# A planned opening in which GpSimd waits for VectorE's preceding instruction on the shared port, with another operation for the softmax sum's epsilon and new plan constants

## The chip, the core and the metric

The kernel runs on one core of one Trainium2 chip. Its engines are TensorE (PE in the profile, its weight loads PEld), VectorE (DVE), ScalarE (ACT), GpSimd (POOL) and SyncE (SP, which here only issues transfers). The metric is the device time of one execution in microseconds, as a median of several runs.

## What is computed

Windowed attention over 8 batches of 8 heads, 576 positions and 64 columns, and behind it a feed-forward block over all 4608 tokens:

```python
scores = scale * np.matmul(q, k.transpose(0, 1, 3, 2))
...
mask = (rel >= 0) & (rel < window)                 # window = 128
scores = np.where(mask, scores + bias[None], -1000000000.0)
scores = scores - np.max(scores, axis=-1, keepdims=True)
attn = np.exp(scores)
attn = attn / (np.sum(attn, axis=-1, keepdims=True) + 1e-09)
return np.matmul(attn, v).astype(np.float32)
...
h = x @ w_in                                       # 512 -> 2048
g = h * (1.0 / (1.0 + np.exp(-1.702 * h)))
return (g @ w_out).astype(np.float32)              # 2048 -> 512
```

## The kernel before

**Products.** Data are fp32. Apart from batch 0's attention, each product is made of three products of fp32r parts: an operand is rounded ("high" part) and the remainder is kept as a "low" part (names `K`, `Q`, `VV`, `xl`, `gl`, `pl`, and the second half of a weight tile `w`). So each operand takes a cast (`copy_on`, L439) on ACT or DVE and a subtraction (`less_on`, L442) on POOL or DVE. Weights come from HBM as raw words and are decoded first: two ACT instructions (L515, L517), two DVE ones (L519, L522), then cast and subtraction.

**Attention.** A unit is two blocks of 128 query rows (or one of 64). `scores` makes s on PE (L693 in batch 0, L696 behind it), `biased` (L711, DVE) adds mask and slope and finds the minimum, `exponents` (L723, ACT) makes exp in place and lets ACT add up each row, so that the sum lies in `sums`. `normal` adds 1e-9 to the sums (L732, DVE tensor_scalar), takes the reciprocal (L734) and multiplies the rows with it (L743 on ACT, L745 on DVE or POOL). `flip` transposes on PE (L766), `high` and `low` empty that, `mix` multiplies with v (L805, L811) and `sum_up` writes x. In batch 0 the tiles `work`, `turned` and `numbers` (minima, sums and reciprocals of 8 heads) lie in places that later hold weights.

**Feed-forward.** A job takes 256 tokens through 16 slices of the hidden width: `up` makes h (L880), ACT makes tanh (L888), DVE the gate (L889), then `gh` and `gl`, and `down` adds into `acc` (L904). The first job stops after eight slices while weights still arrive, and is finished as the third.

**The order.** All this is first recorded as operations with an engine, a cost in ns, buffers and dependences (`Plan.add`). Some may go to either of two or three engines (`ways`). [...] The constants on top steer it: how late an engine may be before another gets the work (`LAX`), how far weights are fetched (`FETCH_AHEAD`), at which tick the first weight is decoded (`DECODE_TICK`), behind which exponent later decodes stand (`GATE`). The order comes out as the program's order on each engine. On the chip each engine takes its instructions in this order, and semaphores hold them for data alone: nothing holds POOL to the planned order against DVE. Where PE would have nothing to do in the plan, `spin` (L486) puts dummy products of the identity, up to the first operation on `acc0`. What the plan doesn't reach is emitted by `rest` in the order in which it was recorded.

Of the kernel before, what the change touches and what calls it, by code (L numbers as in the profile page):

```python
# [14 lines left out]
AF = mybir.ActivationFunctionType  # L15
ALU = mybir.AluOpType
PSUM = bass.MemoryType.PSUM

# [3 lines left out]
P = 128  # L22
# [10 lines left out]
SCALE = 0.125  # L33
BIG = 3.0e38
FAR = 1.0e37
DEPTH = 3
FETCH_AHEAD = 5
DECODE_AHEAD = 1
F0 = 8
SLACK = 2  # L40
DECODE_TICK = 7
AHEAD = 3000
GATE = 6
READY = {"PE": 1600, "DVE": 4400, "ACT": 700, "POOL": 2700, "SP": 700}
HOP = {"PE": 220, "ACT": 60, "DVE": 60, "POOL": 60, "SP": 60}
CUT = 130000
WARM = 7000
LAX = {"w": 1500, "hi": 800, "lo": 2000, "gl": 150, "cast": 300, "xl": 300, "p": 300}
RATE = 330
# [136 lines left out]


class Part:

# [21 lines left out]
class Op:  # L211


    def __init__(self, n, eng, run, ns, lag, port):
        self.n, self.eng, self.run, self.ns, self.lag, self.port = n, eng, run, ns, lag, port
        self.ways = {eng: (ns, port)}
        self.waits, self.next, self.ready, self.opens, self.bufs = 0, [], 0, [], []
        self.bytes = 0
        self.start = None
        self.before = 0  # L220


class Plan:
# [56 lines left out]
    def order(self, until):  # L280

        free = dict(READY)
        port = 0
        wire, landed = 0, []
# [12 lines left out]
        while True:  # L297
            best = None
            for e in ENGINES:
# [21 lines left out]
                if pick:  # L321
                    at = max(pick[0], port) if pick[2].ways[e][1] else pick[0]
                    if best is None or (at, pick[0]) < best[:2]:
                        best = (at, pick[0], pick[2], e)
# [15 lines left out]
            if op.port:  # L340
                port = at + op.ns
            end = at + op.ns + (30 if op.eng == "POOL" else op.lag)
            if op.bytes:
# [56 lines left out]
def tile_kernel(ctx: ExitStack, tc: tile.TileContext, q0, k0, v0, qT, kT, v, w_in, w_out, out):  # L400
# [61 lines left out]
    bias = [const.tile([P, 2 * P], BF16, name=f"bias{h}") for h in range(H)]  # L462

    def tables():


        make_identity(nc, ident)
        rel_i = raw.tile([P, 2 * P], I32, name="rel_i", tag="rq_0")
        nc.gpsimd.iota(rel_i, pattern=[[-1, 2 * P]], base=P, channel_multiplier=1)
# [77 lines left out]
    def home(shape, name):  # L547
        return buf(const, shape, F32, homes.pop(), name=name)
# [108 lines left out]
    def small(u, i, name):  # L657
        if first(u):
            return Part(numbers, (u.n, i), lambda t: t[:, 3 * u.n + i])
        return buf(att, [P, 2], F32, name, 3)  # L660

    def scores(u):
# [34 lines left out]

        add("PE", run, ns, 165, r=reads if u.whole else [u.Q, u.K1, u.K2], w=[u.s], chain="scores")

# [18 lines left out]
    def exponents(u):  # L718
        u.sums = small(u, 1, "sums")
        for e, b in enumerate(u.blocks):  # L720
            def run(e=e, b=b):
                live = b.p.t[:b.rows, b.live:b.end]
                nc.scalar.activation(  # L723
                    live, live, AF.Exp, bias=u.mins.t[:b.rows, e:e + 1], scale=-1.0,
                    accum_out=u.sums.t[:b.rows, e:e + 1])
            gates.append(add(
                "ACT", run, 300 + 0.8 * (b.end - b.live), 95, r=[u.mins.key_at(e)], w=[b.p.key_at(), u.sums.key_at(e)], chain="exp"))

    def normal(u, on_act=False):
        u.rec = small(u, 2, "rec")  # L730
        rows, ne = u.blocks[0].rows, len(u.blocks)
        add("DVE", lambda: nc.vector.tensor_scalar(u.rec.t[:rows, :ne], u.sums.t[:rows, :ne], 1e-9, None, ALU.add),  # L732
            70, 90, r=[u.sums.key_at()], w=[u.rec.key_at()], port=True, chain="rec")
        add("DVE", lambda: nc.vector.reciprocal(u.rec.t[:rows, :ne], u.rec.t[:rows, :ne]),  # L734
# [250 lines left out]
    turned = [home([P, 2, 4 * P], f"turned{i}") for i in range(4)]  # L985
    numbers = home([P, 24, 2], "numbers")
    load_part(0, T, "ACT")
# [67 lines left out]
    def emit(op):  # L1055
        op.run(op.eng) if len(op.ways) > 1 else op.run()

    done = plan.order(CUT)
# [64 lines left out]
```

## Time and profile before

| | |
|---|---|
| runs | 1058.71, 1064.49, 1058.6 us; median 1058.71 |
| profiled execution | 1059.04 us, its span 1057.3 us |
| PE busy | 1046.5 us, 99% of the span |
| DVE, ACT, POOL busy | 717.9, 612.5, 590.2 us |
| DVE, ACT, POOL busy, first 130 us | 112.9, 113.2, 64.3 us |
| DMA, first 40 us | 306 to 410 GB/s; 75 GB/s over the span |

The profile is one execution. Busy time is time in which an engine has an instruction under way; for PE the ends are modelled, so full windows can hold waits. A row of groups gives line, engine, operation, the tiles out<-in, the shapes, the count, then busy us and mean ns of one, then the idle time ahead of them and what ended it. A row of the waits reads: who <- for whom: us in total, times, longest.

### The profile page before, as it was taken

What the parts mean: (1) busy time and instruction counts of PE and PEld (TensorE: products, weight loads), DVE (VectorE), ACT (ScalarE), POOL (GpSimd) and SP (SyncE); (2) the same over time, 40 slices, a digit from 0 to 9 for tenths busy, and PEclk for the clock granted to TensorE, in tenths of its full rate; (3) what the DMA queues carried; (4) which work ended last, traced back from release to release, by engine and by line L of the source; (5) the groups of instructions that cost most, each with busy time, mean ns of one, the idle gap of its engine ahead of it and who ended that gap; (6) DMA issues with size and microseconds to landing.
All of it is one profiled execution on the core that took longest, in us unless ns stands there. A gap on an engine that the chain in (4) does not pass through costs nothing.

```text
span 1057.3 us, 21848 instructions
## 1 busy us (share of the span) xinstructions
PE 1046.5 (99%) x7054; PEld 941.5 (89%) x7054; DVE 717.9 (68%) x2327; ACT 612.5 (58%) x1823; POOL 590.2 (56%) x877
## 2 busy tenths in 40 slices
PE   9999999999999999999999999999999999999998
PEld 5778889998989999999999998999999999999987
DVE  7889988789887868544767677766878586413221
ACT  7988975666666665534555555655665565322222
POOL 3455666676776665544555666655766565323232
PEclk9999999999999999999999999999999999999999
DMA  9712333323332222211222223222322120000000
GB/s 351 293 56 90 122 88 87 83 82 100 83 94 68 84 69 58 72 43 29 67 63 60 73 62 87 67 68 59 87 67 85 54 81 18 20 1 21 1 21 21
DMA packets 88035, 80.21 MB, mean 76 GB/s; under 512 B 41776, under 2 KB 78128, under 8 KB 87920
## 3 DMA queue, kind: packets, MB, share of 16 engines
q1 hardware_dynamic: 82448, 68.84, 22.1%
q10 hardware_dynamic: 5472, 9.96, 2.6%
q8 instruction: 56, 0.92, 0.4%
q14 instruction: 59, 0.48, 0.2%
HBM read 69.34 MB, written 9.44 MB: 75 GB/s over the span
## 4 chain that ended last, share of the span: by engine, by line
PE 93%; DMA 3%; DVE 2%; issue 1%; POOL 1%; ACT 1%; SPq 0%; DVEq 0%; POOLq 0%
PE h_ps L880 37%; PE acc L904 37%; PE x_ps L811 5%; PE s_ps L696 5%; PE t_ps L766 5%; DMA rw<-w_in 1%; PE x_ps L805 1%; DMA v<-v 1%; PE s_ps L693 1%; DMA rw<-w_out 1%; POOL w L442 0%; DVE pb L745 0%; SPq L416 0%; DVE rec L732 0%; DVE pb L711 0%
## 5 line engine op out<-in xcount | busy, mean ns | idle before, releaser
L880 PE MATMUL h_ps<-xh,w 128*128 128x256 f32 x2304 | 368.1, 284 | 1.3 <-DVE g L889 1.1
L442 POOL TENSOR_TENSOR gl<-g,gh 128x256 fp32r<-128x256 f32 x275 | 206.3, 751 | 270.5 <-ACT gh L439 210.3
L880 PEld LDWEIGHTS h_ps<-xh,w 128*128 128x128 f32 x2304 | 327.0, 188 | 29.0 <-DVE g L889 2.1
L904 PE MATMUL acc<-w,gh 128*128 128x512 f32 x1152 | 325.7, 399 | 0.0
L889 DVE SCALAR_TENSOR_TENSOR g<-g,h_ps 128x256 f32<-128x256 f32 x288 | 119.2, 414 | 179.6 <-ACT g L888 178.3
L888 ACT ACTIVATE g<-h_ps 128x256 f32<-128x256 f32 x288 | 109.7, 381 | 201.2 <-PE h_ps L880 184.3
L904 PEld LDWEIGHTS acc<-w,gh 128*128 128x128 f32 x1152 | 195.8, 188 | 25.9 <-issue 0.3
L439 ACT CAST gh<-g 128x256 fp32r<-128x256 f32 x288 | 116.7, 405 | 145.8 <-DVE g L889 135.6
L880 PE MATMUL h_ps<-xl,w 128*128 128x256 f32 x1152 | 194.3, 280 | 0.0
L904 PE MATMUL acc<-w,gl 128*128 128x512 f32 x576 | 187.0, 400 | 0.0
L880 PEld LDWEIGHTS h_ps<-xl,w 128*128 128x128 f32 x1152 | 163.9, 188 | 6.3
L442 POOL TENSOR_TENSOR K<-rk,K 128x384 fp32r<-128x384 f32 (+1 forms) x139 | 126.8, 912 | 73.1 <-ACT Q L439 18.0
L723 ACT ACTIVATE pb<-pb,mins 128x256 f32<-128x256 f32 (+3 forms) x276 | 134.0, 487 | 48.0 <-DVE mins L711 46.3
L711 DVE CUSTOM_DVE_ANT_0 pb<-s_ps,bias 128x256 f32<-128x256 f32 (+2 forms) x304 | 109.3, 378 | 10.7 <-PE s_ps L696 4.4
L745 DVE TENSOR_SCALAR pb<-pb,rec 128x256 f32<-128x256 f32 (+2 forms) x251 | 109.2, 469 | 3.5
L442 POOL TENSOR_TENSOR Q<-rq,Q 64x256 fp32r<-64x256 f32 (+1 forms) x140 | 96.2, 687 | 23.4 <-DVE g L889 3.9
L904 PEld LDWEIGHTS acc<-w,gl 128*128 128x128 f32 x576 | 93.8, 188 | 9.8 <-issue 0.3
L766 PE MATMUL t_ps<-ident,pb 128*128 128x128 f32 (+2 forms) x524 | 94.6, 272 | 0.7 <-DVE pb L745 0.7
L696 PE MATMUL s_ps<-K,Q 128*128 128x256 f32 (+1 forms) x504 | 90.5, 290 | 0.5 <-DVE mins L711 0.4
L732 DVE TENSOR_SCALAR rec<-sums 128x2 f32<-128x2 f32 (+2 forms) x156 | 48.1, 308 | 62.5 <-ACT pb L723 61.4
L785 DVE TENSOR_TENSOR pl<-t_ps,ph 128x512 fp32r<-128x512 f32 (+2 forms) x140 | 84.4, 604 | 4.7 <-ACT ph L439 4.1
L696 PEld LDWEIGHTS s_ps<-K,Q 128*128 128x128 f32 x504 | 74.1, 189 | 6.1 <-DVE mins L711 0.6
(95 smaller groups left out, 1268.6 us busy)
## 6 DMA issues: line engine op xcount, KB each, us to landing
rk<-kT SPq DMA_DIRECT2D x84, 192.0 KB, 2.3
rq<-qT SPq DMA_DIRECT2D x112, 128.0 KB, 2.2
out<-o ACTq DMA_DIRECT2D x36, 256.0 KB, 2.1
rw<-w_in SPq DMA_DIRECT2D x16, 512.0 KB, 8.7
rw<-w_out SPq DMA_DIRECT2D x16, 512.0 KB, 9.6
rk<-kT SPq DMA_DIRECT2D x56, 128.0 KB, 2.0
rv<-v SPq DMA_DIRECT2D x100, 64.0 KB, 2.0
rq<-qT SPq DMA_DIRECT2D x28, 64.0 KB, 1.9
```

What stands on the lines that cost most here:

```text
L439: (nc.scalar.copy if e == "ACT" else nc.vector.tensor_copy)(dst, src)
L442: (nc.gpsimd if e == "POOL" else nc.vector).tensor_tensor(dst, a, b, ALU.subtract)
L696: nc.tensor.matmul(to, u.Q.t[:, q], ks.t[:, k], start=(z == 0), stop=(z == 1))
L711: add("DVE", lambda b=b, e=e, head=head, ra=ra, rb=rb, cs=cs: nc.vector.tensor_tensor_reduce(b.p.t[ra:rb, cs:b.end], u.s.t[ra:rb, e, cs:b. ...
L723: nc.scalar.activation(live, live, AF.Exp, bias=u.mins.t[:b.rows, e:e + 1], scale=-1.0, accum_out=u.sums.t[:b.rows, e:e + 1])
L745: (nc.gpsimd if on == "POOL" else nc.vector).tensor_scalar(live, live, rec, None, ALU.mult)
L766: nc.tensor.transpose(u.t.t[:c.n, w:w + b.rows], b.p.t[:b.rows, col:col + c.n], ident[:b.rows, :b.rows])
L785: add("DVE", lambda m=m, a=a, z=z: nc.vector.tensor_tensor(u.pl.t[:m, a:z], u.t.t[:m, a:z], u.ph.t[:m, a:z].bitcast(F32), ALU.subtract), d ...
L880: nc.tensor.matmul(h.t, w.t[:, z, k * P:(k + 1) * P], x[k].t, start=(part == 0 and k == 0), stop=(part == 2 and k == NC - 1))
L888: add("ACT", lambda: nc.scalar.activation(g.t, h.t, AF.Tanh, scale=0.851), act_psum(T), r=[h], w=[g], shift=-NEXT)
L889: add("DVE", lambda: nc.vector.scalar_tensor_tensor(g.t, g.t, 1.0, h.t, ALU.add, ALU.mult), dve_one(T), r=[h], w=[g], shift=-NEXT)
L904: nc.tensor.matmul(acc.t, g.t[:, t * P:(t + 1) * P], w.t[:, z], start=(f == self.f0 and n == 0), stop=(f == self.f1 - 1 and n == 2))
```

## The change

Four things are changed.

1. `order` remembers the DVE operation on the port that it placed last (`asked`). The first POOL port operation placed behind it starts no earlier than its end plus `BEHIND` = 160 ns in the plan, and in the program gets a semaphore wait on it (`emit`). This holds for the planned part only.
2. Sums and the 1e-9 stand side by side: `sums` gets a second column, set once by two POOL memsets to 1e-9, ACT writes the sum beside it, and a DVE `tensor_reduce` adds the two columns, in place of the tensor_scalar. In the plan this operation no longer counts as one on the port. It is used in the whole program. For all but the first units of batch 0, the sums lie in three fixed slots of one tile (`totals`, class `Fixed`).
3. Scores of odd heads in the first units are booked with 40 ns on PE and 540 ns until their result, where it was their own cost and 165.
4. The constants `FETCH_AHEAD`, `DECODE_TICK`, `GATE` and `LAX` have other values.

```diff
-FETCH_AHEAD = 5
+FETCH_AHEAD = 3
-DECODE_TICK = 7
+DECODE_TICK = 2
+BEHIND = 160
-GATE = 6
+GATE = 10
-LAX = {"w": 1500, "hi": 800, "lo": 2000, "gl": 150, "cast": 300, "xl": 300, "p": 300}
+LAX = {"w": 600, "hi": 800, "lo": 500, "gl": 300, "cast": 100, "xl": 300, "p": 900}
@@ Plan.order
-        port = 0
+        port, asked = 0, None
                     at = max(pick[0], port) if pick[2].ways[e][1] else pick[0]
+                    if e == "POOL" and asked:
+                        at = max(at, asked.start + asked.ns + BEHIND)
             if op.port:
                 port = at + op.ns
+                if op.eng == "DVE":
+                    asked = op
+                elif asked:
+                    op.behind, asked = asked, None
@@ tile_kernel
+    totals = const.tile([P, 3, 2, 2], F32, name="totals")
+        nc.gpsimd.memset(totals[:, :, :, 1], EPS)
+        nc.gpsimd.memset(numbers.t[:, :, 1:3, 1], EPS)
@@ small
-            return Part(numbers, (u.n, i), lambda t: t[:, 3 * u.n + i])
+            return Part(numbers, (u.n, i), lambda t: t[:, u.n, 1:3] if i == 1 else t[:, u.n, i])
+        if i == 1:
+            return Fixed(plan, "sums", 3, lambda at: totals[:, at])
@@ scores
-        add("PE", run, ns, 165, r=reads if u.whole else [u.Q, u.K1, u.K2], w=[u.s], chain="scores")
+        add("PE", run, 40 if early(u) else ns, 540 if early(u) else 165, r=reads if u.whole else [u.Q, u.K1, u.K2], w=[u.s], chain="scores")
@@ exponents
-                    accum_out=u.sums.t[:b.rows, e:e + 1])
+                    accum_out=u.sums.t[:b.rows, e, 0:1])
@@ normal
-        add("DVE", lambda: nc.vector.tensor_scalar(u.rec.t[:rows, :ne], u.sums.t[:rows, :ne], 1e-9, None, ALU.add),
-            70, 90, r=[u.sums.key_at()], w=[u.rec.key_at()], port=True, chain="rec")
+        add("DVE", lambda: nc.vector.tensor_reduce(u.rec.t[:rows, :ne], u.sums.t[:rows, :ne], AX.X, ALU.add),
+            75, 90, r=[u.sums.key_at()], w=[u.rec.key_at()], chain="rec")
@@ emit
+        if op.port and op.start is not None:
+            on = nc.vector.engine if op.eng == "DVE" else nc.gpsimd.engine
+            op.made = next(i for i in reversed(nc.cur_bb.bb.instructions) if i.engine == on)
+            if op.behind:
+                tc.add_manual_dep(op.made, op.behind.made.name, mybir.DependencyInfo(
+                    mybir.DependencyClass.Sync, mybir.DependencyReason.DATA))
```

What this does to the order is seen best on POOL, where the weights of the third to the fifth slice are split. `w` is a weight tile (its subtraction), `wc` the decoded weight, `gl` the gate's low part, `pb` a block of probabilities that is normalised; in brackets stand the engines or transfer queues whose semaphores an instruction waits for. Before:

```order
L442 TENSOR_TENSOR w_2_0_550<-wc_533,w_2_0_550 128x512 [waits DMAHW5_49,Activation_49]
L442 TENSOR_TENSOR w_2_0_575<-wc_565,w_2_0_575 128x512 [waits DMAHW6_49,Activation_49]
L442 TENSOR_TENSOR gl_607<-g_537,gh_599 128x256 [waits PE_49,Activation_49]
L442 TENSOR_TENSOR w_3_0_643<-wc_628,w_3_0_643 128x512 [waits DMAHW7_49,DVE_49]
L442 TENSOR_TENSOR K_0_678<-rk_321,K_0_646 128x384 [waits DMAHW2_49,Activation_49]
L442 TENSOR_TENSOR gl_708<-g_634,gh_697 128x256 [waits PE_49,Activation_49]
L442 TENSOR_TENSOR w_4_0_744<-wc_731,w_4_0_744 128x512 [waits DMAHW1_49,Activation_49]
```

and after:

```order
L464 TENSOR_TENSOR w_2_0_623<-wc_605,w_2_0_623 128x512 [waits DMAHW6_49,DVE_49,Activation_49]
L464 TENSOR_TENSOR w_3_0_658<-wc_648,w_3_0_658 128x512 [waits DMAHW7_49,DVE_49]
L773 TENSOR_SCALAR pb_642<-pb_642,rec_666 128x256 [waits DVE_49,PE_49,Activation_49]
L464 TENSOR_TENSOR w_3_0_699<-wc_688,w_3_0_699 128x512 [waits DMAHW0_49,DVE_49,Activation_49]
L464 TENSOR_TENSOR gl_739<-g_673,gh_732 128x256 [waits DVE_49,PE_49]
L464 TENSOR_TENSOR w_4_0_762<-wc_752,w_4_0_762 128x512 [waits DMAHW1_49,Activation_49]
```

Five of these six rows now wait for DVE, one of seven did before; one subtraction of slice 2 has gone to DVE and a normalisation has come.

On DVE the first unit of batch 0 shows the sum's operation. The ISA rows are `biased` and its read of the minimum. Before:

```order
L711 ISA work_0_135,numbers_136<-s_h_132,bias_75 128x128 [waits DVE_49,PE_49]
L711 ISA numbers_136 128x1
L732 TENSOR_SCALAR numbers_136<-numbers_136 128x2 [waits Activation_49]
L711 ISA work_0_135,numbers_136<-s_h_132,bias_75 128x256
L711 ISA numbers_136 128x1
L734 RECIPROCAL numbers_136<-numbers_136 128x2 [waits DVE_49]
L745 TENSOR_SCALAR work_0_135<-work_0_135,numbers_136 128x128 [waits DVE_49]
```

and after:

```order
L739 ISA work_0_139,numbers_91<-s_h_136,bias_75 128x128 [waits DVE_49,PE_49]
L739 ISA numbers_91 128x1
L739 ISA work_0_139,numbers_91<-s_h_136,bias_75 128x256
L739 ISA numbers_91 128x1
L760 TENSOR_REDUCE numbers_91<-numbers_91 128x2 [waits Activation_49]
L762 RECIPROCAL numbers_91<-numbers_91 128x2 [waits DVE_49]
L773 TENSOR_SCALAR work_0_139<-work_0_139,numbers_91 128x128 [waits DVE_49]
```

The new operation stands one `biased` later, directly ahead of its reciprocal.

On PE, at the scores of the first two heads (`s_ps` and `s_h`), before:

```order
L693 MATMUL s_ps_127<-k_0_107,q_0_109 128x256
L693 MATMUL s_h_132<-k_0_107,q_0_109 128x128
L693 MATMUL s_h_132<-k_0_107,q_0_109 128x256
L693 MATMUL s_ps_141<-k_0_107,q_0_109 128x128
L693 MATMUL s_ps_141<-k_0_107,q_0_109 128x256
```

and after:

```order
L721 MATMUL s_ps_131<-k_0_111,q_0_113 128x256
L721 MATMUL s_h_136<-k_0_111,q_0_113 128x128
L721 MATMUL s_h_136<-k_0_111,q_0_113 128x256
L512 LDWEIGHTS ident
L512 MATMUL idle<-ident 128x256
```

Five such dummy products now stand between the first pair of heads and the second; over the whole program there are 76 where there were 66.

More of the change, by code (lines that the diff above doesn't have):

```diff
@@ L16 @@
 ALU = mybir.AluOpType
+AX = mybir.AxisListType
 PSUM = bass.MemoryType.PSUM
@@ L34 @@
 BIG = 3.0e38
+EPS = 1e-9
 FAR = 1.0e37
 DEPTH = 3
-FETCH_AHEAD = 5
+FETCH_AHEAD = 3
 DECODE_AHEAD = 1
@@ L185, in key_at, with __init__, t @@
         return self, sub
+class Fixed(Buf):
+    def __init__(self, plan, tag, slots, place):
+        super().__init__(plan, None, None, None, tag, slots)
+        self.place = place
+    @property
+    def t(self):
+        return self.place(self.at)
 class Part:
@@ L220, in __init__ @@
         self.before = 0
+        self.behind = self.made = None
 class Plan:
@@ L729, in normal @@
     def normal(u, on_act=False):
-        u.rec = small(u, 2, "rec")
+        u.rec = small(u, 3, "rec")
         rows, ne = u.blocks[0].rows, len(u.blocks)
-        add("DVE", lambda: nc.vector.tensor_scalar(u.rec.t[:rows, :ne], u.sums.t[:rows, :ne], 1e-9, None, ALU.add),
-            70, 90, r=[u.sums.key_at()], w=[u.rec.key_at()], port=True, chain="rec")
+        add("DVE", lambda: nc.vector.tensor_reduce(u.rec.t[:rows, :ne], u.sums.t[:rows, :ne], AX.X, ALU.add),
+            75, 90, r=[u.sums.key_at()], w=[u.rec.key_at()], chain="rec")
         add("DVE", lambda: nc.vector.reciprocal(u.rec.t[:rows, :ne], u.rec.t[:rows, :ne]),
@@ L985, in tile_kernel @@
     turned = [home([P, 2, 4 * P], f"turned{i}") for i in range(4)]
-    numbers = home([P, 24, 2], "numbers")
+    numbers = home([P, H, 4, 2], "numbers")
     load_part(0, T, "ACT")
```

## The prediction

> **What bounds the kernel now.** I read the page's busy shares and its chain, then the windows, then the waits of PE, and last the DVE groups of the opening. Busy shares and the chain by engine:
>
> ```profile
> PE 1046.5 (99%) x7054; PEld 941.5 (89%) x7054; DVE 717.9 (68%) x2327; ACT 612.5 (58%) x1823; POOL 590.2 (56%) x877
> PE 93%; DMA 3%; DVE 2%; issue 1%; POOL 1%; ACT 1%; SPq 0%; DVEq 0%; POOLq 0%
> ```
>
> PE is the bound as a mean. The windows show where it is not alone (columns: length, then busy us of PE, PEld, DVE, ACT and POOL, the granted clock, the DMA share and GB/s):
>
> ```profile
> 40.00:50.00 10.00, 9.84 (x59) 7.65 (x58) 9.34 (x28) 9.89 (x25) 4.21 (x4) 1.00 0.56 221
> 120.00:130.00 10.00, 9.95 (x73) 9.11 (x72) 9.69 (x30) 9.85 (x30) 5.92 (x8) 1.00 0.20 49
> 0.00:130.00 130.00, 126.44 (x796) 98.50 (x797) 112.89 (x351) 113.15 (x308) 64.25 (x76) 0.99 0.51 183
> 260.00:520.00 260.00, 259.18 (x1777) 238.43 (x1776) 183.06 (x606) 148.87 (x457) 157.89 (x244) 1.00 0.24 67
> ```
>
> From 260 to 520 us DVE has 77 of 260 us idle and ACT 111, so there only PE counts, and nothing in this change removes PE work. In the first 130 us DVE and ACT both are busy for 113 us, while POOL is busy for 64. What PE waits for directly is small, in the first 140 us and behind them:
>
> ```profile
> PE s_ps L693 <- DVE numbers L711: 1.0, 1, 1.0
> PE s_ps L693 <- DVE mins L711: 0.7, 1, 0.7
> PE h_ps L880 <- POOL w L442: 0.2, 1, 0.2
> PE h_ps L880 <- DVE g L889: 1.1, 2, 0.8
> PE x_ps L811 <- DVE xf L851: 0.8, 2, 0.4
> PE t_ps L766 <- DVE pb L745: 0.7, 1, 0.7
> ```
>
> The first three are the opening's, the last three are of the rest. More is hidden in fillers, the dummy products of L486, which stand where the planner expects PE to wait, and in modelled matmul ends. The fillers of the first 30 and the next 30 us, and ten in a row:
>
> ```profile
> 0.00:30.00 30.00, 8.47 (x55) 5.42 (x55) 0.94 0.97 357
> 30.00:60.00 30.00, 1.55 (x11) 0.91 (x11) 1.00 0.53 210
> 24.68 1.27 PE L486 MATMUL idle<-ident 128*128 128x256 bf16 x10
> 25.78 0.27 PE L766 MATMUL t_ps<-ident,work 128*128 128x128 f32 x1
> ```
>
> Ten start within 25.78 - 24.68 = 1.10 us, 0.11 us each, so the 66 fillers are some 7.3 us. Whatever this change gives must come out of the opening: out of these fillers and out of the lateness of DVE and ACT.
>
> **The port.** What the new wait is about can be seen at 50.8 us, in the timeline:
>
> ```profile
> 42.50 0.75 DVE L439 CAST w<-wc 128x512 fp32r<-128x512 f32 x2
> 50.83 1.28 POOL L442 TENSOR_TENSOR w<-wc,w 128x512 fp32r<-128x512 f32 x1 [2.86 <-ACT w L439]
> 50.87 1.52 DVE L439 CAST w<-wc 128x512 fp32r<-128x512 f32 x1
> ```
>
> and in the chain of work that ended last:
>
> ```profile
> 50.96 1.43 DVE w L439
> ...
> 52.79 1.14 PE s_ps L693 x6
> ```
>
> Two casts in a row take 0.75 us, 0.375 each. The one at 50.87 began 0.04 us behind a POOL subtraction and took 1.52, until just after POOL's end at 52.11. It lost 1.15 us, and it is on the chain: PE's scores start behind it at 52.79 (the 0.7 us wait above). POOL itself had idled 2.86 us before and was in no hurry.
>
> **The change part by part.** First the size of all such losses on DVE in the first 145 us, from the groups kept apart by form (mean ns behind the comma):
>
> ```profile
> L522 DVE SCALAR_TENSOR_TENSOR wc<-rw,w_ps 128x512 int32<-128x512 int32 x32 | 21.4, 675 | 0.0
> L889 DVE SCALAR_TENSOR_TENSOR g<-g,h_ps 128x256 f32<-128x256 f32 x24 | 9.9, 412 | 0.9 <-ACT g L888 0.7
> L442 DVE TENSOR_TENSOR gl<-g,gh 128x256 fp32r<-128x256 f32 x13 | 8.5, 653 | 0.9 <-PE acc L904 0.9
> L442 DVE TENSOR_TENSOR w<-wc,w 128x512 fp32r<-128x512 f32 x8 | 6.0, 749 | 0.0
> L439 DVE CAST w<-wc 128x512 fp32r<-128x512 f32 x10 | 5.6, 568 | 0.0
> L732 DVE TENSOR_SCALAR rec<-sums 128x2 f32<-128x2 f32 x16 | 3.6, 227 | 1.4 <-ACT pb L723 1.2
> L734 DVE RECIPROCAL rec<-rec 128x2 f32<-128x2 f32 x16 | 2.5, 155 | 0.0
> L732 DVE TENSOR_SCALAR numbers<-numbers 128x2 f32<-128x2 f32 x8 | 2.4, 305 | 0.5 <-ACT work L723 0.5
> L442 DVE TENSOR_TENSOR xl<-x,xh 128x256 fp32r<-128x256 f32 x2 | 2.0, 978 | 0.0
> L745 DVE TENSOR_SCALAR pb<-pb,rec 128x192 f32<-128x192 f32 x4 | 1.8, 448 | 0.0
> L745 DVE TENSOR_SCALAR pb<-pb,rec 64x192 f32<-64x192 f32 x1 | 1.4, 1365 | 0.0
> ```
>
> L889 and L522 are two-operand operations of the same shapes as gl, xl and w that read PSUM, and never stretch. Above them lie gl with 13 x (653 - 412) = 3.1 us, xl with 2 x (978 - 412) = 1.1, w with 8 x (749 - 675) = 0.6, the casts with 10 x (568 - 375) = 1.9, one normalisation with 1365 - 448 = 0.9. That is 7.6 us. The sum's addition of 1e-9, against the reciprocal of the same two columns: 16 x (227 - 155) + 8 x (305 - 155) = 2.3 us.
>
> (a) The addition becomes a tensor_reduce. The trace has no such instruction. From below, it costs a reciprocal's 155 ns; two more elements to read cost (412 - 155) / 254 = 1 ns each by the slope between L734 and L889. From above, it costs the addition's 227 and 305 and gains nothing. I take 157. What comes back is then all of the 2.3 us on DVE. One such loss stands on the chain, behind the planned part:
>
> ```profile
> 143.47 0.79 DVE rec L732
> 144.28 0.18 DVE rec L734
> ```
>
> That is 0.6 us beyond a bare one. I take 1.0 us for the end time, between 0 and 2.3. In the rest of the program 132 more such additions get shorter, but DVE idles there and PE's waits for it sum to 2.6 us in the three rows above. I take 0, and if they all went, 2.6.
>
> (b) POOL waits for DVE's preceding port instruction. In the order, 49 of the planned POOL rows wait for DVE where 18 did. [...] Bounds are 1.1 and 7.6 us; I take a third, 2.5, because DVE is over nine tenths busy in the two windows shown, yet PE's direct waits for it in the opening are 1.7 us. The price is on POOL: 31 added waits, each with whatever is queued behind it there, subtractions for w and gl that PE's products need. POOL idles 66 of the first 130 us, and PE waited for it 0.2 us. I take 0.5 us. If that cover were gone, 31 waits of about the 0.45 us of a DVE port operation would be 14 us on POOL, and a third of them on PE's path 4.7.
>
> [...]
>
> (c) The new constants move work. In the order ACT has 17 instructions fewer, DVE 16 more (10 subtractions come from POOL, 16 copies and casts from ACT, 10 normalisations leave for POOL and ACT), POOL 3 more, two of them memsets. Means of what leaves ACT:
>
> ```profile
> L439 ACT CAST gh<-g 128x256 fp32r<-128x256 f32 x21 | 8.5, 403 | 0.6 <-DVE g L889 0.5
> L439 ACT COPY turned<-t_ps 128x384 f32<-128x384 f32 x6 | 2.8, 475 | 2.4 <-PE t_ps L766 2.4
> ```
>
> 17 x 0.42 = 7.1 us off ACT. ACT is at 9.85 or more in two of the fourteen windows of 10 us up to 140 us, and only there do I count it: 7.1 x 2 / 14 = 1.0 us of gain. The bounds are 4 us of gain (over half reaches the end) and 5.2 us of loss (DVE, below). The transfers cost nothing: SP's queue holds the same loads in the same order for its first 78 rows. The two memsets on POOL come ahead of the mask tables:
>
> ```profile
> 2.91 1.70 DVE L478 TENSOR_SCALAR bias<-rel 128x256 bf16<-128x256 f32 x8 [0.97 <-POOL rel L473]
> 0.74 0.20 POOL masks.py:197 MEMSET ident<- 128x128 f32 x1 [0.29 <-POOLq L1119]
> 5.33 0.29 DVE L711 CUSTOM_DVE_ANT_0 work<-s_ps,bias 128x128 f32<-128x128 f32 x1 [0.71 <-PE s_h L693]
> ```
>
> At 0.2 us each at most, 0.4 us are hidden: its tables are made at 4.61, and DVE then waits 0.71 us for PE's first scores. Ten more fillers, 76 for 66, would be 1.1 us of PE, but fillers stand where PE waits anyway; 0, at worst 1.1.
>
> **The sum.** -1.0 - 2.5 + 0.5 - 1.0 = -4.0 us. The profiled execution took 1059.0 us (1057.3 in the span, 1.7 around it), 0.3 above the runs' median of 1058.7; so 1055.0 on its own scale and 1054.7 as a median. What a measurement of this kernel tells from no change is about 1%, 10.6 us: below 1048.1 or above 1069.3.
>
> **The rivals.**
>
> No change, 1057 to 1060, about 1058.5. [...] Against it: the cast at 50.87 is on the chain and POOL's idle time of 2.86 us in front of it wasn't. This also covers the case that the change doesn't do what it says, because the added waits are nearly always over when POOL gets its data.
>
> DVE becomes the bound of the opening, slower, about 1064. Ten subtractions at about 0.6 us (between the 412 and the 675 ns above) and 16 copies and casts at about the 0.375 of a bare cast come to DVE, 10 normalisations at 0.45 leave it: 6.0 + 6.0 - 4.5 = 7.5 us more. At 9.69 of 10 in 120 to 130 us it has no room there. If the collisions stay and only the 2.3 us of (a) come back, DVE ends 5.2 us later: 1058.7 + 5.2 = 1063.9. It decides once DVE's windows up to 130 us stand at 9.7 or more; for it speaks that row, against it the 17 us that DVE idles over the 130.
>
> The opening follows its plan and all stretching goes: 9.9 us of DVE, 1058.7 - 9.9 = 1048.8. For it: DVE and ACT are both nearly full and feed each other, so that one late instruction makes the other late. Against it: most of the stretched groups can be cases in which POOL was rightly first.
>
> **How the numbers follow.** The forecast, 1052 to 1057, has 0.50; no change 0.22; DVE or POOL late, above 1060, 0.14; nearly all recovered, below 1052, 0.14. The range goes from 1049.0, the full recovery, to 1061.5, half of the slower case's 5.2 us above the median, and leaves about 0.15 out. Faster by over 1% needs more than the whole port loss, 0.05; slower by over 1% would need twice DVE's added work, 0.02; within 1%, 0.93.
>
> **What would show it.** In the changed profile: tensor_reduce at 150 to 165 ns in the opening and behind it; the DVE groups of gl, w and the cast nearer to 412, 675 and 375; more POOL idle time released by DVE, and PE's waits for POOL still under 1 us; ACT's windows at 40 and 120 us below 9.8; PE's span from 260 us on as before. I am wrong if the stretched groups stay as they are while the time falls (then moved work did it), if PE comes to wait for POOL's w or gl by microseconds, or if DVE's windows reach 9.7 and the end is later.

## The result and the profile after

The changed kernel took 1052.82 us as a median of six runs (1052.34 to 1053.83), the kernel before 1059.43 on the same chip (six runs). The ratio is 0.9932 with a 95% interval of 0.9913 to 0.9951. One execution of the kernel before took 1064.49 us and the other five 1058.2 to 1060.2, while none of the changed kernel's stands apart, so the ratio says a little more than the medians. By these it is 6.6 us faster, where 4.0 were forecast; the time lies in the range, and most of the gain comes from a place that the prediction had ruled out.

Busy shares and the chain by engine of the changed kernel (profiled execution 1052.34 us, span 1050.6):

```profile
PE 1041.9 (99%) x7064; PEld 938.8 (89%) x7064; DVE 695.9 (66%) x2343; ACT 613.7 (58%) x1806; POOL 586.7 (56%) x880
PE 96%; DVE 2%; ACT 1%; issue 0%; POOL 0%; DVEq 0%; POOLq 0%; ACTq 0%
```

PE is busy for 4.6 us less, with ten products more. DVE is busy for 22 us less. Two stretches of the prediction, and one near the end of the program:

```profile
40.00:50.00 10.00, 10.00 (x63) 7.63 (x61) 8.56 (x28) 9.11 (x24) 5.12 (x6) 1.00 0.53 211
120.00:130.00 10.00, 9.90 (x67) 8.60 (x66) 9.83 (x35) 8.75 (x27) 5.93 (x10) 1.00 0.21 56
950.00:1040.00 90.00, 90.00 (x587) 81.86 (x586) 22.69 (x49) 25.59 (x65) 27.07 (x37) 1.00 0.04 13
```

and the last of these in the kernel before:

```profile
950.00:1040.00 90.00, 90.00 (x581) 81.29 (x580) 22.26 (x48) 25.29 (x64) 26.82 (x37) 1.00 0.03 13
```

The last rows are the surprise. Near the end there is no attention, both kernels run the same products in the same order, PE is full, and the clock is 1.00. Still PE begins 587 products in 90 us, where it began 581: 1% more. What PE waits for, in the first 140 us (first row) and behind them:

```profile
PE idle L512 <- POOL ident masks.py:199: 1.4, 1, 1.4
...
PE t_ps L794 <- DVE pb L773: 0.9, 2, 0.6
PE s_ps L724 <- DVE mins L739: 0.9, 2, 0.7
PE h_ps L908 <- DVE xh L461: 0.5, 1, 0.5
PE x_ps L839 <- DVE xf L879: 0.2, 1, 0.2
```

The wait for the identity, 1.4 us, is there in both kernels. The opening's other waits of 1.9 us are gone; those behind it sum to 2.5 us, about what they were (2.6). And the DVE groups of the first 145 us that answer to the prediction's:

```profile
L464 DVE TENSOR_TENSOR w<-wc,w 128x512 fp32r<-128x512 f32 x13 | 10.7, 824 | 1.4 <-ACT w L461 1.4
L464 DVE TENSOR_TENSOR gl<-g,gh 128x256 fp32r<-128x256 f32 x14 | 6.1, 434 | 0.4 <-ACT gh L461 0.3
L461 DVE CAST w<-wc 128x512 fp32r<-128x512 f32 x6 | 2.7, 457 | 0.0
L760 DVE TENSOR_REDUCE rec<-totals 128x2 f32<-128x4 f32 x15 | 2.3, 150 | 0.3 <-ACT pb L751 0.2
```

gl fell from 653 to 434 ns, the cast from 568 to 457, while w rose from 749 to 824. The tensor_reduce takes 150 ns.

Where the gain arises shows when the starts of the same product are compared. The h products (L880, now L908) are 3456 in both kernels:

| h product | start before, us | start after, us | lead, us |
|---|---|---|---|
| 300th | 141.47 | 139.79 | 1.7 |
| 800th | 307.48 | 306.22 | 1.3 |
| 1000th | 369.95 | 367.96 | 2.0 |
| 2000th | 655.41 | 651.47 | 3.9 |
| 3000th | 943.45 | 938.10 | 5.4 |
| last | 1048.56 | 1041.92 | 6.6 |

Under 2 us come from the opening; 4.6 us come steadily behind the 1000th product, where the change edits nothing but an operation of DVE's. The same run of 12 h products in the last stage, first before (eight with the high part, four with the low):

```profile
946.37 1.10 PE L880 MATMUL h_ps<-xh,w 128*128 128x256 f32 x8
947.32 0.62 PE L880 MATMUL h_ps<-xl,w 128*128 128x256 f32 x4
947.78 1.09 PE L904 MATMUL acc<-w,gh 128*128 128x512 f32 x4
```

and after:

```profile
940.96 1.09 PE L908 MATMUL h_ps<-xh,w 128*128 128x256 f32 x8
941.89 0.62 PE L908 MATMUL h_ps<-xl,w 128*128 128x256 f32 x4
942.34 1.08 PE L932 MATMUL acc<-w,gh 128*128 128x512 f32 x4
```

From the first start to acc it is 1.41 us before and 1.38 after, 117.5 against 115 ns for one product of the same shape.

What differs there is only where the tiles lie. `totals` takes 64 bytes ahead of the weights, and three small `sums` buffers are gone behind them. So in bytes of a partition, read from the built programs, the weight tiles begin at 192 modulo 256, where they began at 128, and x, xh, xl, g, gh and gl at 128, where they began at 160. The distance from a weight tile to an x or g tile is 192 modulo 256, where it was 32. That was my theory for the bulk of the gain, with the rival that the new operation, waits and order bring it. "Last stage" below is the time from the 3001st of these products (counted from 0) to the last: 104.87 us before, 103.59 after.

### The profile page after: what moved, and what is told of

It reads as the page before. It is cut to its first block, busy times and chain, and to the rows that moved or that the text cites. A ratio compares the mean times of both kernels' runs of the same rounds, so it can differ in the third digit from the quotient of the medians.

```text
span 1050.6 us, 21901 instructions
## 1 busy us (share of the span) xinstructions
PE 1041.9 (99%) x7064; PEld 938.8 (89%) x7064; DVE 695.9 (66%) x2343; ACT 613.7 (58%) x1806; POOL 586.7 (56%) x880
## 4 chain that ended last, share of the span: by engine, by line
PE 96%; DVE 2%; ACT 1%; issue 0%; POOL 0%; DVEq 0%; POOLq 0%; ACTq 0%
PE h_ps L908 38%; PE acc L932 37%; PE t_ps L794 6%; PE x_ps L839 5%; PE s_ps L724 5%; PE s_ps L721 2%; PE x_ps L833 1%; PE idle L512 1%; DVE pb L773 0%; DVE pb L739 0%; PE x_acc L833 0%; DVE xl L464 0%; DVE xh L461 0%; DVE K L461 0%; PE s_h L721 0%
## 5 line engine op out<-in xcount | busy, mean ns | idle before, releaser
L908 PE MATMUL h_ps<-xh,w 128*128 128x256 f32 x2304 | 368.7, 283 | 0.6 <-DVE xh L461 0.5
L908 PEld LDWEIGHTS h_ps<-xh,w 128*128 128x128 f32 x2304 | 327.2, 188 | 27.2 <-DVE xh L461 0.7
L908 PE MATMUL h_ps<-xl,w 128*128 128x256 f32 x1152 | 193.4, 280 | 0.0
L908 PEld LDWEIGHTS h_ps<-xl,w 128*128 128x128 f32 x1152 | 163.3, 188 | 5.6
L464 POOL TENSOR_TENSOR K<-rk,K 128x384 fp32r<-128x384 f32 (+1 forms) x137 | 124.4, 908 | 75.7 <-PE x_ps L839 14.9
L773 DVE TENSOR_SCALAR pb<-pb,rec 128x256 f32<-128x256 f32 (+2 forms) x246 | 100.9, 446 | 3.8
L464 POOL TENSOR_TENSOR VV<-rv,VV 128x128 fp32r<-128x128 f32 (+2 forms) x139 | 66.0, 475 | 27.0 <-ACT VV L461 19.0
```

The lines of the kernel that those rows point to most:

```text
L464: (nc.gpsimd if e == "POOL" else nc.vector).tensor_tensor(dst, a, b, ALU.subtract)
L773: (nc.gpsimd if on == "POOL" else nc.vector).tensor_scalar(live, live, rec, None, ALU.mult)
L908: nc.tensor.matmul(h.t, w.t[:, z, k * P:(k + 1) * P], x[k].t, start=(part == 0 and k == 0), stop=(part == 2 and k == NC - 1))
```

## The experiments

**1. Placement moved by 32 bytes, in both kernels.** The theory at that time was cruder: what counts is whether the x tiles begin at a multiple of 64. An unused tile of 32 bytes ahead of them is all that is added, on a line that exists:

```diff
-    bias = [const.tile([P, 2 * P], BF16, name=f"bias{h}") for h in range(H)]
+    bias = [const.tile([P, 2 * P], BF16, name=f"bias{h}") for h in range(H)]; pad = xp.tile([P, 8], F32, name="pad", tag="pad", bufs=1)
```

In the kernel before (distance 64 now):

> The kernel before, with one unused tile of 32 bytes a partition laid ahead of the feed-forward tiles, so that x, xh, xl, g, gh, gl start at multiples of 64 bytes (as in the changed kernel) and not 32 behind one; the order is the same instruction by instruction. Theory (where these tiles start in memory sets the pace of PE's feed-forward products: 117.2 against 116.0 ns for one of h and 233.2 against 230.3 for one of acc in the two profiles' last 100 us, and about 1 ns in the middle): 3 to 5 us faster, 1054 to 1056. Rival (the pace belongs to the execution or the chip, not to the program): no change, within 1 us.

In the changed kernel (distance 224):

> The changed kernel with the same unused 32 bytes, so that the feed-forward tiles start 32 bytes behind a multiple of 64, as in the kernel before. Theory (place in memory): 3 to 5 us slower than the changed kernel's 1052.8, 1056 to 1058. Rival (execution or chip): 1052 to 1054.

Measured: the kernel before with the tile took 1059.51 us, ratio 1.001 (0.9993 to 1.0027), last stage 105.12 us. The changed one took 1060.36 us, ratio 0.9999 (0.9985 to 1.0013), last stage 105.12 us. The first missed: multiples of 64 are not the rule. The second lost more than expected: 32 unused bytes take away the whole gain of the change. In the same 90 us it begins 578 products, nine fewer than the changed kernel. Its profiled run also had half the clock for 3.4 us at 302 us (0.72 as the mean of 300 to 306 us), which by estimate costs at most half of that, 1.7 us; so of the loss of 7.5 us some 6 at the least are the pace.

**2. The waits alone, and the operation alone, undone.** An operation "on the port" is one that the plan marks with `port=True`, some of POOL's and some of DVE's; it plans no two of them at the same time. That is the planner's booking; the runs show which of DVE's instructions took longer and by how much, and not what the two engines share. Neither edit moves an instruction, and the tiles stay. The waits:

```diff
-            if op.behind:
+            if op.behind and False:
```

> The changed kernel in its own order, but POOL's added semaphore waits on VectorE are not emitted. If the waits give what the prediction's step (b) said (2.5 us less 0.5), 1054 to 1056. Rival (the order alone gives the opening's gain, the waits are nearly always over): 1052 to 1054. Second rival (the waits cost more than they give): below 1052.

The operation (the sum's first column is read, the second is not used):

```diff
-        add("DVE", lambda: nc.vector.tensor_reduce(u.rec.t[:rows, :ne], u.sums.t[:rows, :ne], AX.X, ALU.add),
+        add("DVE", lambda: nc.vector.tensor_scalar(u.rec.t[:rows, :ne], u.sums.t[:rows, :ne, 0], 1e-9, None, ALU.add),
```

> [...] If the operation gives what step (a) said, 1.0 us (0 to 2.3) slower, about 1053.8, with the additions in the opening at 200 ns and more against about 150. Rival (hidden): 1052 to 1053.5.

Measured: without the waits 1053.72 us, ratio 0.995 (0.9937 to 0.9964), so the waits are worth 0.9 us by the medians and 1.9 by the ratios. That is hardly clear of the noise: the intervals of the two ratios overlap, and so do the executions (1053.19 to 1054.68 without, 1052.34 to 1053.83 with the waits). The time is that of the first rival, in which the waits give little. With the old operation 1055.85 us, ratio 0.997 (0.9959 to 0.9982), so the tensor_reduce is worth 3.0 us (4.0 by the ratios); its fastest execution, 1055.09, lies above the slowest of the changed kernel. Without the waits these are DVE's groups in the first 145 us and, last, what PE waits for in the opening beside the identity:

```profile
L464 DVE TENSOR_TENSOR w<-wc,w 128x512 fp32r<-128x512 f32 x13 | 10.2, 783 | 1.3 <-ACT w L461 1.3
L464 DVE TENSOR_TENSOR gl<-g,gh 128x256 fp32r<-128x256 f32 x13 | 6.9, 529 | 0.1
L461 DVE CAST w<-wc 128x512 fp32r<-128x512 f32 x6 | 3.2, 541 | 0.0
L464 DVE TENSOR_TENSOR K<-rk,K 128x256 fp32r<-128x256 f32 x2 | 1.1, 550 | 0.0
...
PE t_ps L794 <- DVE pl L813: 0.6, 1, 0.6
PE s_ps L724 <- POOL gl L464: 0.2, 1, 0.2
```

and K with the waits:

```profile
L464 DVE TENSOR_TENSOR K<-rk,K 128x256 fp32r<-128x256 f32 x2 | 1.8, 906 | 0.0
```

The waits take gl from 529 to 434 ns and the cast from 541 to 457, as the prediction said. But w goes from 783 to 824 and K from 550 to 906. Over the 405 instructions that DVE begins in the first 145 us without the waits, the same instructions take 0.2 us more with them: gl, the casts and the normalisations gain 2.5 us, K, w and xl lose 2.4, the rest is small. So the waits move the stretching on DVE and don't shorten it as a whole. What they do in the profiles is that the last two rows are gone: PE's two waits in the opening, 0.8 us together.

The two profiles with the new and the old operation are 3.6 us apart: 0.7 of it stand at the 300th h product (140 us), 2.3 more have come by the 800th (307 us), and 0.6 behind that. The largest single piece can be read off. With the old operation, on POOL, on DVE and then on PE (in brackets the idle time ahead of an instruction and what ended it):

```profile
296.34 0.74 POOL L464 TENSOR_TENSOR Q<-rq,Q 64x256 fp32r<-64x256 f32 x1
297.35 0.74 POOL L464 TENSOR_TENSOR gl<-g,gh 128x256 fp32r<-128x256 f32 x1
...
296.74 0.56 DVE L760 TENSOR_SCALAR rec<-totals 128x2 f32<-128x2 f32 x1
297.44 0.87 DVE L461 CAST K<-rk 128x384 fp32r<-128x384 f32 x1
298.24 2.10 DVE L773 TENSOR_SCALAR pb<-pb,rec 128x128 f32<-128x128 f32 x2
...
300.21 0.30 PE L794 MATMUL t_ps<-ident,pb 128*128 128x128 f32 x1 [1.96 <-DVE pb L773]
301.07 1.22 PE L724 MATMUL s_ps<-K,Q 128*128 128x256 f32 x4
...
300.90:304.50 3.60, 3.60 (x18) 3.35 (x17) 3.51 (x16) 2.43 (x9) 1.31 (x4) 0.53 0.57 175
```

and the same place with the tensor_reduce:

```profile
294.10 0.74 POOL L464 TENSOR_TENSOR Q<-rq,Q 64x256 fp32r<-64x256 f32 x1
...
294.50 0.16 DVE L760 TENSOR_REDUCE rec<-totals 128x2 f32<-128x4 f32 x1
294.80 0.45 DVE L461 CAST K<-rk 128x384 fp32r<-128x384 f32 x1
295.21 2.22 DVE L773 TENSOR_SCALAR pb<-pb,rec 128x128 f32<-128x128 f32 x2
...
297.49 0.44 PE L794 MATMUL t_ps<-ident,pb 128*128 128x128 f32 x2 [0.65 <-DVE pb L773]
298.18 0.74 PE L724 MATMUL s_ps<-K,Q 128*128 128x256 f32 x4 [0.25 <-DVE mins L739]
```

The old operation comes 0.40 us behind the start of POOL's subtraction for Q and takes 0.56 us, until shortly behind its end. That makes the cast behind it meet POOL's next subtraction, 0.87 us in place of 0.45. So the normalisation starts 1.50 us behind the operation in place of 0.71, PE waits 1.96 us in place of 0.65, and within 1 us after that wait the clock falls to half for 3.4 us (0.53 in the window from 300.9 to 304.5). The tensor_reduce too began 0.40 us behind the start of that POOL subtraction, and took 0.16. All this is worth some 0.7 us: ahead of the wait the same products start 2.2 us later than in the changed kernel, at 308 us 3.0 us later. The half clock adds nothing to that. The scores at 301.07 are 2.89 us late against 298.18, and the next ones, behind the half clock, 2.90 (307.88 against 304.98); in the changed kernel PE stands for another 1 us in between. So the 3.0 us are not one fall of the clock, and most of the lag had come before it, in smaller steps.

**3. Placement alone, the order of before.** In the kernel before, the pools `xp` and `ffn` are made ahead of `const`, and `const` gets 64 unused bytes, so that weights begin at 192 and x at 128 modulo 256 as in the changed kernel; no instruction is changed.

```diff
+    xp = ctx.enter_context(tc.tile_pool(name="xp", bufs=1))
+    ffn = ctx.enter_context(tc.tile_pool(name="ffn", bufs=1))
...
-    xp = ctx.enter_context(tc.tile_pool(name="xp", bufs=1))
-    ffn = ctx.enter_context(tc.tile_pool(name="ffn", bufs=1))
...
-    bias = [const.tile([P, 2 * P], BF16, name=f"bias{h}") for h in range(H)]
+    bias = [const.tile([P, 2 * P], BF16, name=f"bias{h}") for h in range(H)]; pad = const.tile([P, 16], F32, name="pad")
```

> The kernel before, instruction for instruction in its own order; only the tiles lie elsewhere: the feed-forward tiles (x, xh, xl, g, gh, gl, wc) at multiples of 128 bytes and the weights 64 behind one, as in the changed kernel, where before had 32 behind and 0. Theory (where the operands start, counted modulo 128 bytes, sets PE's pace): h at 116.0 ns and acc at 230.3 in the last 100 us as in the changed kernel, 4 to 5 us faster than before, 1054 to 1056. Rival (it takes the changed kernel's full addresses or its order): pace as before, 117.2 and 233.2, and 1058 to 1060.5.

Measured: 1054.92 us, ratio 0.9961 (0.9941 to 0.998), last stage 103.59 us as in the changed kernel.

```profile
950.00:1040.00 90.00, 90.00 (x585) 81.79 (x584) 22.73 (x49) 25.80 (x66) 26.92 (x37) 1.00 0.04 13
```

So 4.9 us under the 1059.79 of the kernel before in the same comparison (4.1 by the ratio) come without the change, from the places of the tiles. The profiles say the same behind the opening: from the 300th h product to the last it is 907.1 us in the kernel before, 902.4 with new places alone and 902.1 in the changed kernel, 4.7 of 5.0 us. The opening of this profile isn't that of the kernel before, though the program's order is: PE's first products run at half pace for longer, for instance the four

```profile
6.02 1.64 PE L693 MATMUL s_ps<-k,q 64*128 64x128 f32 x4 [0.72 <-DVE numbers L711]
```

which took 0.89 us there, and the full clock is on its record from 13.9 us only. Its 300th h product starts at 142.45 us, 1 us later than before.

Then both starts at 128, distance 0: in the kernel before by making the pool `att` last, in the changed kernel by the same and by a place for `totals` in `att`.

```diff
-    att = ctx.enter_context(tc.tile_pool(name="att", bufs=1))
     xp = ctx.enter_context(tc.tile_pool(name="xp", bufs=1))
     ffn = ctx.enter_context(tc.tile_pool(name="ffn", bufs=1))
+    att = ctx.enter_context(tc.tile_pool(name="att", bufs=1))
```

> The kernel before in its own order with the feed-forward tiles at multiples of 128 bytes and the weights left at multiples of 128. If both operands add their part (x off a multiple of 128: 2.4 to 3.1 ns for a product of h; weights 64 off: 1.2 ns, as the four profiles so far can be read): h at about 114.8 ns, 6 to 8 us faster than before, 1051 to 1054. Rival (a fixed distance between the two operands matters, not each one's start): no better than before, 1058 to 1060.

> The changed kernel in its own order, with weights and feed-forward tiles all at multiples of 128 bytes. If the parts add: h at about 114.8 ns against 116.0, 2 to 5 us faster than the changed kernel, 1048 to 1051. Rival (distance): 1052 to 1060.

Measured: 1062.15 us for the kernel before (ratio 1.0027, 1.0009 to 1.0045) and 1060.03 for the changed one (1.0002, 0.999 to 1.0014), last stage 105.58 us in both. A good place for x and a good place for weights, each by itself, is not the rule either; the distance between them was left.

**4. PE by itself, 64 pairs of starts.** All other engines stand idle, so that nothing but PE reads the tiles.

```diff
+        for w in ws:
+            for x in xs:
+                for n in range(4):
+                    for k in range(12):
+                        nc.tensor.matmul(hs[n % 2], w[:, k % 8 * P:(k % 8 + 1) * P], x[:, k % 4 * 256:(k % 4 + 1) * 256], start=k == 0, stop=k == 11)
```

> This kernel computes nothing of the reference: it leaves the whole computation out and runs TensorE alone on the kernel's two kinds of long product, 48 per pair of operands of the h kind (a 128-column weight tile stationary, 256 columns of x moving) and then 24 per pair of the acc kind (x stationary, 512 columns of weights moving), with eight x tiles and eight w tiles that begin at 128, 160, 192, 224, 0, 32, 64 and 96 modulo 256 (xa to xh, wa to wh), all other engines idle. Theory 'distance': the mean start-to-start time of the h products depends on (x - w) modulo 256 and is equal along a diagonal of the 8 by 8 table: shortest at 192 (near 114 to 115 ns), longest at 0 (near 119 ns), 32 near 117; between 2 and 4% from best to worst; the acc kind likewise by about 1%. Rival 'pair': the table has no such diagonals, but single pairs stand out. Rival 'contention': with the other engines idle the table is flat to 0.5 ns, since the placement only decides how PE's reads fall against the others' accesses.

Measured, mean ns from start to start, for the eight pairs of each distance (lowest to highest pair):

| distance from w to x, modulo 256 | h kind, ns | acc kind, ns |
|---|---|---|
| 0 | 119.8 to 119.9 | 226.9 to 227.7 |
| 32 | 117.8 to 117.9 | 233.0 to 233.1 |
| 64 | 117.8 to 117.9 | 233.0 to 233.5 |
| 96 | 119.8 to 120.0 | 234.0 to 234.3 |
| 128 | 118.6 to 118.8 | 232.2 to 233.5 |
| 160 | 117.3 to 118.7 | 233.1 to 233.9 |
| 192 | 113.6 to 117.9 | 228.7 to 229.3 |
| 224 | 118.2 to 118.3 | 233.3 to 233.5 |

Four neighbouring groups of 48 in the timeline (`wd` begins at 224; `xb`, `xc`, `xd`, `xe` at 160, 192, 224 and 0; the first of four rows of 12 of each, so a difference of starts is 48 products):

```profile
176.68 1.53 PE L82 MATMUL ha<-xb,wd 128*128 128x256 f32 x12
...
182.14 1.58 PE L82 MATMUL ha<-xc,wd 128*128 128x256 f32 x12
...
187.81 1.60 PE L82 MATMUL ha<-xd,wd 128*128 128x256 f32 x12
...
193.56 1.58 PE L82 MATMUL ha<-xe,wd 128*128 128x256 f32 x12
```

5.46, 5.67 and 5.75 us: 113.7 ns at distance 192, 118.1 at 224, 119.8 at 0. No other engine is at work here, so PE's own two operands are enough to change its pace. Along a distance the h kind is equal to 0.2 ns at six of eight. At 160 and 192 it takes one of two values, 117.3 or 118.6 and 113.6 or 117.8; at 192 only the pairs 224 and 160, 96 and 32 (w and x) have the lower. So the distance is most of the rule and not all of it.

The sweep doesn't reproduce all of the kernels' gain either. The changed kernel's own pair, 192 and 128, takes 117.9 ns for h in the sweep, as much as the pair of the kernel before, 128 and 160; only the acc kind is faster for it, 229.3 against 233.0. In the kernels' last stage both are: from one h product with the high part to the next it is 117.2 ns before and 116.0 in the changed kernel, from an acc product to whatever follows 233.2 and 230.3, and each kind makes about half of the 1.28 us. So the acc half is shown with PE alone. For the h half nothing here separates PE's own reading from what the other engines read at the same time. Over all kernels the mean for h falls from distance 0 (119.3) over 224 (118.4), 64 (117.9) and 32 (117.2) to 192 (116.0, at both pairs of starts).

**5. The same distance at other places.** The changed kernel with 32 unused bytes in `const`, ahead of both: weights at 224, x at 160, the pair that was fastest in the sweep.

```diff
-    bias = [const.tile([P, 2 * P], BF16, name=f"bias{h}") for h in range(H)]
+    bias = [const.tile([P, 2 * P], BF16, name=f"bias{h}") for h in range(H)]; pad = const.tile([P, 8], F32, name="pad")
```

> The changed kernel with 32 bytes of unused tile ahead of the weights, so that weights begin at 224 and the x and g tiles at 160 modulo 256: both moved, their distance (192) kept. Theory 'distance': the pace stays that of the changed kernel, last stage (3001st to 3455th h product) 103.4 to 103.8 us, time 1052 to 1053.5. Finer theory from the sweep, where this very pair of starts held 113.6 ns for the h kind and the changed kernel's pair 117.9, at 229.3 for the acc kind in both: last stage 102.9 to 103.3, time 1049.5 to 1051.5. Rival 'pair': the good pace belongs to 192 and 128 alone: last stage 104.9 to 105.6, time 1057 to 1060.

Measured: 1052.97 us, ratio 0.9938 (0.992 to 0.9955), last stage 103.59 us. The distance held: the same 32 bytes that cost 7.5 us between weights and x cost nothing ahead of both. The finer forecast of another 2 us failed; among other products this pair is no better than 192 and 128. Of the five distances that whole kernels had (0, 32, 64, 192, 224), the changed kernel's has the shortest last stage, and no version has a lower median.

**6. The old constants, and the parts under them.** The changed program with the four constants of before and with the old booking of the early scores; tiles at distance 192 as in the changed kernel. This is not the order of before, since the rules of the planner stay changed.

```diff
-FETCH_AHEAD = 3
+FETCH_AHEAD = 5
-DECODE_TICK = 2
+DECODE_TICK = 7
-GATE = 10
+GATE = 6
-LAX = {"w": 600, "hi": 800, "lo": 500, "gl": 300, "cast": 100, "xl": 300, "p": 900}
+LAX = {"w": 1500, "hi": 800, "lo": 2000, "gl": 150, "cast": 300, "xl": 300, "p": 300}
-        add("PE", run, 40 if early(u) else ns, 540 if early(u) else 165, r=reads if u.whole else [u.Q, u.K1, u.K2], w=[u.s], chain="scores")
+        add("PE", run, ns, 165, r=reads if u.whole else [u.Q, u.K1, u.K2], w=[u.s], chain="scores")
```

> The changed kernel's waits and tensor_reduce with the planner's old constants and the old booking of the odd heads' scores; feed-forward tiles at multiples of 128 bytes and weights 64 behind, as in the changed kernel. If the new constants give what the two profiles show up to the 300th product of h: 1 to 3 us slower than the changed kernel, 1054 to 1056, at the changed kernel's pace in the last 100 us. Rival (the constants give nothing): 1052 to 1053.5.

Measured: 1057.21 us, ratio 0.9971 (0.9949 to 0.9993). The new constants and the booking are worth 4.4 us, where the waits, the operation and the places are given. That is more than the 1 to 3 us expected, and it isn't what they are worth against the order of before, which at the same places took 1054.92 (experiment 3): under the new rules the old constants give an order that is slower than that by 2.3 us. In the profile it has fallen behind by 311 us: its 800th h product starts 5.1 us later than in the changed kernel, and its last 4.5. Then, in this order, once with the old operation and once without the waits (the edits of experiment 2):

> The changed program with the old constants and the old booking of the early scores (the run with old constants took 1057.2), and with the tensor_scalar again in place of the tensor_reduce; the waits stay, placement as in the changed kernel. If the operation is worth 3.0 us in any order, as in the changed order, 1060.2; if those 3.0 us were one mishap of that order (half the clock for 3.4 us at 301 us), 1057.2 to 1058. Rival: the waits are what makes this order slower than the order of before at the same placement (1054.9): then the time stays above 1057 here, whatever the operation.

> The changed program with the old constants and the old booking, with the tensor_reduce but without the waits; placement as in the changed kernel. If the waits are worth 0.9 us in any order, 1058.1; if the waits are what costs this order its 2.3 us against the order of before at the same placement, 1055 to 1056.

Measured: with the old operation 1060.39 us, ratio 0.9996 (0.9979 to 1.0012); without the waits 1059.34 us, ratio 1.0003 (0.9988 to 1.0017). The operation is worth 3.2 us here by the medians (0.25% by the ratios), the waits 2.1 (0.3%). So the operation's 3.0 us are no mishap of one order: behind the opening the clock falls nowhere in this one. And the rival that the waits cost this order its 2.3 us against experiment 3 missed: without them it is slower.

## Why the prediction was right, and where it was wrong

**The total.** -4.0 was forecast; -6.6 came, of which the places of the tiles alone make -4.9 (experiment 3) and all that the prediction costed some -2.1 (1052.82 against 1054.92; 3.1 us by the ratios; the kernel before differs by 0.4 us between the two comparisons). The range held for a reason that isn't in the text, which is luck. (Its ends, 1049.0 and 1061.5, are 0.2 off the 1048.8 and 1061.3 that its sums give, and the fillers are some 8 us and not 7.3, since the first ten took 0.21 us each and not 0.11; nothing rests on either.)

**The step that failed** is "nothing in this change removes PE work", with its consequence "Whatever this change gives must come out of the opening" and the sign "PE's span from 260 us on as before". The work is the same, but its pace isn't: the last stage, with identical products, took 103.59 us in place of 104.87. The diff had the cause in it, `totals` in the pool `const` and three buffers less in `att`; I costed instructions and never looked at where the tiles behind an added one come to lie.

**(a) The operation** was put at 1.0 us, 0 of it behind the opening; it is worth 3.0. The duration was right: 150 ns in the first 145 us for the forecast 157. What failed is "DVE idles there", from which I took 0 behind 145 us, with 2.6 as the end of the range. The rows for the two-column operation behind 140 us, before:

```profile
L732 DVE TENSOR_SCALAR rec<-sums 128x2 f32<-128x2 f32 x105 | 40.1, 382 | 58.5 <-ACT pb L723 57.9
```

and after:

```profile
L760 DVE TENSOR_REDUCE rec<-totals 128x2 f32<-128x4 f32 x105 | 16.3, 156 | 58.6 <-ACT pb L751 57.9
```

24 us of DVE time, ten times the opening's 2.3, and the addition is the head of a chain (reciprocal, normalisation, transposition on PE), so that a part of it reached PE though DVE had idle time elsewhere. I had read only the opening's row. For the opening itself the 1.0 us was about right: 0.7 stand at the 300th h product.

**(b) The waits** were put at 2.0 us net. They are worth 0.9, hardly clear of the noise (2.1 under the old constants). The term that failed is the gain of 2.5 us, taken as a third of the stretching on DVE: in the same order the waits take nothing off DVE as a whole, since K, w and xl stretch by what gl and the casts no longer lose (experiment 2). Most of the fall of gl from 653 ns came with the new order, which has 529 without the waits. The price of 0.5 us can't be seen: apart from the identity at the start PE waits for POOL nowhere in the opening. The sign "more POOL idle time released by DVE" came only against the same order without the waits: the rows of the first 130 us sum to 22.1 us there, to 25.9 with the waits, and to 25.6 in the kernel before. The sign of w missed: 824 ns, away from 675.

**(c) The constants** were put at 1.0 us; 4.4 us were measured against the old ones under the new rules, which is another comparison than the forecast's and can't size its term. ACT's windows at 40 and 120 us fell to 9.11 and 8.75 as forecast. DVE stands at 9.83 in 120 to 130 us, above the point from which the slower rival was to decide, and PE is not late there: a full window by itself decided nothing.

**What is open.** The parts measured in the changed order (0.9, 3.0 and 4.4) sum to 8.3, the whole beside the places to 2.1 to 3.1. If they simply added, the rest of the change under the old constants (the planner's new rules, the two memsets, the three fixed slots for the sums) would have cost 5 or 6 us; no run has that part alone, and the parts need not add. The 2.1 us also hold what the clock did in the first 14 us, which differs between profiles of one order (experiment 3), and no run separates that. Nor do the runs show what in PE's reading makes the distance count, or why the h product gains in the kernel and not in the sweep. What makes the clock fall, and what decides when it becomes full, is open too.

## What to carry to other kernels

An edit that adds or drops a small tile moves all tiles behind it, and that can be worth as much as the edit or more (here 4.9 of 6.6 us): compare the starts of identical work far from the change before explaining a gain by the change. When an edit is judged by a few tenths of a per cent, pad it so that the hot operands keep their places, or measure the old kernel with the new places. Weigh a cheaper small operation by the chain that it heads in the whole program, not by how idle its engine is as a mean (here it was worth 3.0 us, where 1.0 was forecast).

## What the runs showed of the hardware

In the sweep's 64 pairs of starts, with no other engine at work, the pace of the same fp32 product depends on the distance of its two operands' starts modulo 256 bytes: 119.9 ns at 0 and 113.6 at best, 5%, for 128 columns by 256; 226.9 to 234.3 ns for 128 by 512, where 0 is the fastest. At two of the eight distances the starts themselves count too (for 128 by 256, 117.3 to 118.7 ns at 160 and 113.6 to 117.9 at 192).

The granted clock fell to half for one stretch of 3.4 us in several profiles: with the old operation at 301 us (0.53 as the mean of 300.9 to 304.5 us), behind a wait of PE of 1.96 us (above), and in the kernel before at 8.4 us, where its products had stood 0.96 us for DVE. The rows, with the clock of that stretch:

```profile
6.25 0.89 PE L693 MATMUL s_ps<-k,q 64*128 64x128 f32 x4 [0.96 <-DVE numbers L711]
...
8.40:11.80 3.40, 3.40 (x16) 1.96 (x14) 2.58 (x19) 3.06 (x13) 0.65 (x1) 0.50 1.02 411
```

The changed kernel has five dummy products where PE had stood 0.96 us, and waits 0.65 us where it had waited 1.96, and in its profile the clock falls at neither (1.00 from 5.2 us to the last product). But the wait alone doesn't decide it: the changed kernel with 32 bytes ahead of x (experiment 1) has the same order and at most 0.64 us of wait in the place of the 1.96 us, and its clock fell there, at 301.8 us.

The full clock came late at the start of some executions. PE's first dummy products start 0.21 us apart, later ones 0.11. In the traces' record of the clock the full clock begins at 5.0 us in the kernel before and 5.2 in the changed one, at 13.9 with the order of before in other places (experiment 3), and at 24.9 in the profile of experiment 6 without the waits, which took 1064.45 us: there four products of turned and v still took 1.54 us at 22.7 us, where the kernel before needed 0.86.

The tensor_reduce of two columns took 156 ns as a mean of 105, at times beside a POOL subtraction (0.16 us at 294.50, above), where the tensor_scalar took 382. Behind 140 us all 133 of it, those of one column among them, took 134 to 159 ns, where the tensor_scalar took 131 to 780.

DVE's other instructions differ in their spread by kind. In the first 145 us of the kernel before, the 24 gates (L889) took 399 to 423 ns and the 32 second DVE steps of the decoding (L522) 657 to 689, while gl took 410 to 1302 ns, the subtraction for w 674 to 1083 and the cast of w 409 to 1517.
